# Writing the experts' gates and token numbers from GpSimd's queue instead of SyncE's

## Chip, cores and metric

The kernel runs on one core of a Trainium2 chip. The metric is the device time of one execution in microseconds (us); lower is better. The core has five engines that run their own instruction streams in order: PE (TensorE, matrix products), DVE (VectorE), ACT (ScalarE), POOL (GpSimd) and SP (SyncE, which here only starts transfers). SP and POOL can both start DMA transfers; an instruction that waits for a semaphore holds up everything behind it on its engine.

## What is computed

Three layers in a row: a linear attention with decays, a mixture of experts that sends each token to one of eight experts, and a dense layer of two matrices.

```python
for t in range(S):                                   # S = 768, 4 x 8 heads of 48
    state = alpha[:, :, t, :, None] * state + einsum('bhd,bhe->bhde', k[:, :, t], v[:, :, t])
    y[:, :, t] = einsum('bhd,bhde->bhe', q[:, :, t], state)
x = y.transpose(0, 2, 1, 3).reshape(3072, 384)
...
expert_idx = argmax(logits, axis=1)                  # logits from normalized x and expert_emb
gate_w = probs[arange(N), expert_idx]
for e in range(8):
    mask = expert_idx == e
    h = maximum(x[mask] @ w1[e], 0.0)                # 384 -> 1024
    out[mask] = gate_w[mask, None] * (h @ w2[e])     # 1024 -> 384
...
h = x @ w_in                                         # 384 -> 2048
return maximum(0.01 * h, h) @ w_out                  # 2048 -> 384
```

## The kernel before

Matrix products run in float16 with each float32 operand split into a high and a low half (`w1h`, `w1l` and so on), so that a product of two operands is three matmuls.

**Attention** (up to about 178 us) also routes: each token's row of 388 floats (its features, a norm, its gate, its token number) is scattered by POOL (L598) into `bucket`, an array in HBM with one region for each expert. The weights of expert 0 are loaded and split there too.

**The scheduled experts' stage** (about 178 to 426 us) treats 432 tokens of each expert, e = 0 to 7. For each expert:

- `gather(e)` (L834, L831): SP fetches the rows from `bucket` into `xg`, of which there are two buffers, xg0 for even experts (printed xg_1923) and xg1 for odd ones (xg_1924). So gather(e+2) must wait until all readers of expert e's rows are through.
- `put_meta(e)` (L848 to L851): two columns of `xg`, gate and token number, are written to `meta` in HBM, at a place that a register holds (`offi`, the experts' offsets, loaded by L848). The first transfer writes 384 rows of 8 bytes, the second the last 48. Since the place is known only at run time, each such transfer waits until the one before it has landed; and the first one waits until the rows of `xg` have landed.
- `block(e, n)`: ACT (L882) and DVE (L883) scale and split the rows into `xs`, and SP starts DMA transposes (L885) into `xt`, also two buffers.
- `weights(e+1, j)`: eight pieces of 128 x 768 floats, each fetched by SP (L894, into one of five `wstage` buffers) and split by ACT (L899) and DVE (L900). `double` does the same with a quarter of `w_in` or `w_out`, from 64-bit floats, through L916 to L922.
- `up(e, f)`: 72 matmuls (L940 to L942), then `hh` by ACT (L945) and `hl` by DVE (L946). `down(e, d)`: 72 matmuls (L965 to L967), then `x2h` by ACT (L971) and `x2l` by DVE (L972).

The order on each engine is made ahead of time by `Plan`: every step is added with an engine, a cost, what it reads and writes, and a due time; a list scheduler places them, and the instructions are issued in the order of planned starts. A step's cost and engine thus shift all others. For transfers the plan counts bytes over a rate plus a landing time. Of the waits inside `put_meta`, between its two transfers and from one expert's to the next, the plan knows nothing.

**The dense layer** (426 us to the end) reads `meta` back once (L1018), multiplies, and scatters the rows of the output by POOL (L799).

Of the kernel before, what the change touches and what calls it, by code (L numbers as in the profile page):

```python
# [21 lines left out]
P = 128  # L22
# [3 lines left out]
D = H * HD  # L26
NT = B * S
# [7 lines left out]
CAP = 432  # L35
# [135 lines left out]
def body(ctx, tc, qT, kT, aT, v, emb, tau, w1, w2, w_in, w_out, out):  # L171
    nc = tc.nc
# [7 lines left out]
    meta = dram.tile([X2, 2], F32, name="meta")  # L180
# [21 lines left out]
    offi = const.tile([P, E], I32, name="offi")  # L202
# [68 lines left out]
    with tc.tile_pool(name="at", bufs=1) as rt, \  # L271
# [59 lines left out]
        plan = Plan()  # L331
        NU = B * NP
        V, S_, T_, G_, Q_ = "DVE", "ACT", "PE", "POOL", "SP"
# [468 lines left out]
    with tc.tile_pool(name="mx", bufs=2) as mxp, tc.tile_pool(name="mh", bufs=1) as mhp, \  # L802
# [15 lines left out]
        size = [min(P, CAP - n * P) for n in range(NB)]  # L818
        NF = CAP // P
        plan = Plan(rate=230e3, land=4.0)  # L820
        V, S_, T_, Q_ = "DVE", "ACT", "PE", "SP"
        START, TURN = 20.0, 26.4

        def begin(e):
            return START + TURN * e
# [18 lines left out]
        def put_meta(e):  # L844
            xg = xgs[e % 2]

            def go():
                so = nc.sync.value_load(offi[0:1, e:e + 1], min_val=0, max_val=NT)  # L848
                nc.sync.dma_start(meta[ds(so, NF * P)].rearrange("(n p) c -> p n c", p=P), xg[:, :NF, D + 1:D + 3])
                if CAP % P:  # L850
                    nc.sync.dma_start(meta[ds(so + NF * P, CAP % P)], xg[:CAP % P, NF, D + 1:D + 3])  # L851

            plan.add(Q_, 1.2, go, [("xg", e % 2)], [("meta", e)], at=begin(e) + 4)

        def first_rows(n):
            x, m = xrow[n % 3], size[n]
# [118 lines left out]
        with tc.manual_schedule():  # L975
# [19 lines left out]
            for e in range(E):  # L995
                if e:
                    add(pieces_of(e))
                for f in range(NF1):
                    up(e, f)
                    if e + 1 < E and f < NB:  # L1000
                        block(e + 1, f)
                    if f == 2:
                        put_meta(e)
                    if f == 4 and e + 2 < E:
                        gather(e + 2)
                places(e)
                for d in range(KD):
                    down(e, d)
# [60 lines left out]
    with tc.If(left > 0):  # L1069
        with tc.For_i(0, left, 1) as i, tc.tile_pool(name="ox", bufs=1) as op, \  # L1070
# [7 lines left out]
            xg = op.tile([P, AUG], F32, name="xg")  # L1078
# [51 lines left out]
```

## Time and profile before

| | us |
|---|---|
| median of 3 runs | 814.64 (813.8 to 816.43) |
| the profiled execution | 810.95 |
| its span in the trace | 809.2 |
| PE busy in the span | 769.7 (95%) |
| DVE / ACT / POOL busy | 455.8 / 338.8 / 89.3 |

The profiled execution took 1.75 us more than its span, for what lies around it. PE's busy share is near full over the whole span, and the page's row of 40 slices shows where it is not: behind the first slice, all digits under 9 but the last lie between 162 and 283 us, at the end of the attention and in the first half of the experts' stage. A matmul's duration in the trace is its way through a pipeline, longer than the distance to the next one; so counts and starts tell more than sums of durations. The granted clock of TensorE stands as a share of its full 2.4 GHz; 0.5 is its lower level, 1.2 GHz.

### The profile page before, as it was taken

What the parts mean: (1) busy time and instruction counts of PE and PEld (TensorE: products, weight loads), DVE (VectorE), ACT (ScalarE), POOL (GpSimd) and SP (SyncE); (2) the same over time, 40 slices, a digit from 0 to 9 for tenths busy, and PEclk for the clock granted to TensorE, in tenths of its full rate; (3) what the DMA queues carried; (4) which work ended last, traced back from release to release, by engine and by line L of the source; (5) the groups of instructions that cost most, each with busy time, mean ns of one, the idle gap of its engine ahead of it and who ended that gap; (6) DMA issues with size and microseconds to landing.
All of it is one profiled execution on the core that took longest, in us unless ns stands there. A gap on an engine that the chain in (4) does not pass through costs nothing.

```text
span 809.2 us, 12898 instructions
## 1 busy us (share of the span) xinstructions
PE 769.7 (95%) x5098; PEld 431.5 (53%) x5098; DVE 455.8 (56%) x784; ACT 338.8 (42%) x671; POOL 89.3 (11%) x92
## 2 busy tenths in 40 slices
PE   6999999988869799999999999999999999999996
PEld 3777767645435355555554564464465465465453
DVE  9989999747355678887876504603603602602610
ACT  1344536426244567675654404403503503512510
POOL 6121624220000000000000010010000000000000
PEclk8999999999979899999999999999999999999999
DMA  8884945325666689868600000000000000000000
GB/s 304 280 272 128 294 141 184 99 95 131 157 156 159 210 198 251 184 200 226 208 25 2 1 30 10 1 20 20 1 20 20 0 20 20 1 21 20 0 21 23
DMA packets 61666, 84.08 MB, mean 104 GB/s; under 512 B 29848, under 2 KB 40864, under 8 KB 61600
## 3 DMA queue, kind: packets, MB, share of 16 engines
q1 hardware_dynamic: 58464, 73.69, 32.8%
q0 software_dynamic: 3136, 9.50, 3.0%
q8 instruction: 42, 0.69, 0.4%
q14 instruction: 24, 0.20, 0.1%
HBM read 66.80 MB, written 11.73 MB: 97 GB/s over the span
## 4 chain that ended last, share of the span: by engine, by line
issue 45%; PE 34%; DMA 7%; DVE 6%; POOL 4%; ACT 2%; SPq 1%; POOLq 0%; DVEq 0%; ACTq 0%
PE ps L966 3%; PE ps L967 3%; PE ps L965 3%; PE ps L942 3%; PE ps L941 3%; PE ps L940 3%; PE psc L398 3%; POOL out L799 3%; PE py L417 3%; PE py L449 2%; PE pfill L338 2%; DMA xg<-bucket 2%; DMA wstage<-in_w 2%; DMA meta<-xg 1%; PE ptr L477 1%
## 5 line engine op out<-in xcount | busy, mean ns | idle before, releaser
L782 DVE SCALAR_TENSOR_TENSOR g<-ps,r 128x512 f32<-128x512 f32 x96 | 65.7, 684 | 150.3 <-ACT r L781 150.3
L794 PE MATMUL ps<-woh,gh 128*128 128x384 f16 x384 | 125.2, 326 | 0.0
L795 PE MATMUL ps<-wol,gh 128*128 128x384 f16 x384 | 125.2, 326 | 0.0
L796 PE MATMUL ps<-woh,gl 128*128 128x384 f16 x384 | 125.2, 326 | 0.0
L776 PE MATMUL ps<-x2h,wih 128*128 128x512 f16 x288 | 109.1, 379 | 1.4 <-DVE x2l L972 1.4
L777 PE MATMUL ps<-x2l,wih 128*128 128x512 f16 x288 | 109.2, 379 | 0.0
L778 PE MATMUL ps<-x2h,wil 128*128 128x512 f16 x288 | 109.2, 379 | 0.0
L786 DVE TENSOR_TENSOR gl<-g,gh 128x512 f16<-128x512 f32 x96 | 66.5, 692 | 65.4 <-ACT gh L785 65.4
L785 ACT ACTIVATE gh<-g 128x512 f16<-128x512 f32 x96 | 60.4, 629 | 82.6 <-DVE g L782 82.5
L940 PE MATMUL ps<-xt,w1h 128*128 128x432 f16 x192 | 69.0, 360 | 12.6 <-DVE hl L946 9.2
L798 ACT ACTIVATE osb<-ps,ms 128x384 f32<-128x384 f32 x24 | 13.9, 580 | 159.5 <-PE ps L796 159.5
L965 PE MATMUL ps<-hh,w2h 128*128 128x432 f16 x192 | 67.5, 351 | 2.0 <-ACT hh L945 2.0
L941 PE MATMUL ps<-xt,w1h 128*128 128x432 f16 x192 | 69.0, 359 | 0.0
L942 PE MATMUL ps<-xt,w1l 128*128 128x432 f16 x192 | 68.7, 358 | 0.0
L966 PE MATMUL ps<-hl,w2h 128*128 128x432 f16 x192 | 67.5, 351 | 1.2 <-DVE hl L946 1.2
L967 PE MATMUL ps<-hh,w2l 128*128 128x432 f16 x192 | 67.5, 351 | 0.0
L799 POOL DMA_INDIRECT out<-osb,tki x24 | 23.6, 984 | 352.1 <-ACT osb L798 345.3
L781 ACT ACTIVATE r<-ps 128x512 f32<-128x512 f32 x96 | 55.9, 583 | 10.8 <-PE ps L778 7.9
L338 PE MATMUL pfill<-busy,ones 128*128 128x512 f16 x161 | 51.4, 417 | 1.5 <-POOL ident masks.py:199 1.5
L794 PEld LDWEIGHTS <-gh 128*128 128x128 f16 x384 | 37.6, 98 | 25.1
L795 PEld LDWEIGHTS <-gh 128*128 128x128 f16 x384 | 37.6, 98 | 25.1
L796 PEld LDWEIGHTS <-gl 128*128 128x128 f16 x384 | 37.6, 98 | 24.8
(197 smaller groups left out, 1133.6 us busy)
## 6 DMA issues: line engine op xcount, KB each, us to landing
wstage<-in_w SPq DMA_DIRECT2D x64, 384.0 KB, 5.2
a<-in_aT SPq DMA_DIRECT2D x16, 387.5 KB, 3.6
k<-in_kT SPq DMA_DIRECT2D x16, 384.0 KB, 4.3
q<-in_qT SPq DMA_DIRECT2D x16, 384.0 KB, 6.4
wstage<-in_w_in SPq DMA_DIRECT2D x16, 384.0 KB, 5.1
wstage<-in_w_out SPq DMA_DIRECT2D x16, 384.0 KB, 3.6
v<-in_v SPq DMA_DIRECT2D x8, 576.0 KB, 7.9
xg<-bucket SPq DMA_DIRECT2D x7, 582.0 KB, 5.6
```

Of the source, the lines that this page charges most:

```text
L776: nc.tensor.matmul(ps, wih[:, k, fs], xh[:, k], start=k == 0, stop=False)
L777: nc.tensor.matmul(ps, wih[:, k, fs], xl[:, k], start=False, stop=False)
L778: nc.tensor.matmul(ps, wil[:, k, fs], xh[:, k], start=False, stop=k == KD - 1)
L794: nc.tensor.matmul(ps, ghs[f][:, ts], woh[:, f], start=f == 0, stop=False)
L795: nc.tensor.matmul(ps, ghs[f][:, ts], wol[:, f], start=False, stop=False)
L796: nc.tensor.matmul(ps, gls[f][:, ts], woh[:, f], start=False, stop=f == NF2 - 1)
L940: nc.tensor.matmul(ps, w1h[:, f, k], xt[:, k], start=k == 0, stop=False)
L941: nc.tensor.matmul(ps, w1h[:, f, k], xt[:, KD + k], start=False, stop=False)
L942: nc.tensor.matmul(ps, w1l[:, f, k], xt[:, k], start=False, stop=k == KD - 1)
L965: nc.tensor.matmul(ps, w2h[:, f, cols], hh, start=f == 0, stop=False)
L966: nc.tensor.matmul(ps, w2h[:, f, cols], hl, start=False, stop=False)
L967: nc.tensor.matmul(ps, w2l[:, f, cols], hh, start=False, stop=f == NF1 - 1)
```

## The change

`put_meta` is issued by POOL instead of SP: the load of the offset and both transfers. In the plan it stands on POOL with a cost of 6.0 us, where it stood on SP with 1.2 us. Nothing else is edited; what moves on other engines is the scheduler's doing.

```diff
-        V, S_, T_, Q_ = "DVE", "ACT", "PE", "SP"
+        V, S_, T_, G_, Q_ = "DVE", "ACT", "PE", "POOL", "SP"
...
             def go():
-                so = nc.sync.value_load(offi[0:1, e:e + 1], min_val=0, max_val=NT)
-                nc.sync.dma_start(meta[ds(so, NF * P)].rearrange("(n p) c -> p n c", p=P), xg[:, :NF, D + 1:D + 3])
+                so = nc.gpsimd.value_load(offi[0:1, e:e + 1], min_val=0, max_val=NT)
+                nc.gpsimd.dma_start(meta[ds(so, NF * P)].rearrange("(n p) c -> p n c", p=P), xg[:, :NF, D + 1:D + 3])
                 if CAP % P:
-                    nc.sync.dma_start(meta[ds(so + NF * P, CAP % P)], xg[:CAP % P, NF, D + 1:D + 3])
-
-            plan.add(Q_, 1.2, go, [("xg", e % 2)], [("meta", e)], at=begin(e) + 4)
+                    nc.gpsimd.dma_start(meta[ds(so + NF * P, CAP % P)], xg[:CAP % P, NF, D + 1:D + 3])
+
+            plan.add(G_, 6.0, go, [("xg", e % 2)], [("meta", e)], at=begin(e) + 4)
```

PE's order is the same in both kernels. SP's list is shorter by the eight steps, and its other steps are regrouped. Here SP before, from gather(2) (into xg_1923) through put_meta(2) to the transposes of expert 1 (xt_1926):

```order
L834 DMA xg_1923<-bucket 128x3x388
L831 DMA xg_1923<-bucket 48x388
L848 TENSOR_LOAD offi
L848 ISA x2
L849 ISA
L849 DMA meta<-xg_1923 128x3x2
L851 ISA
L851 DMA meta<-xg_1923 48x2
L885 DMA_TRANSPOSE xt_1926<-xs_1931 128x6x128
L885 DMA_TRANSPOSE xt_1926<-xs_1932 128x6x128
L885 DMA_TRANSPOSE xt_1926<-xs_1933 128x6x128
L894 DMA wstage<-in_w 128x768
```

And SP at the same place of the changed kernel, on to gather(3) (into xg_1924) and the weights behind it:

```order
L885 DMA_TRANSPOSE xt_1926<-xs_1931 128x6x128
L885 DMA_TRANSPOSE xt_1926<-xs_1932 128x6x128
L834 DMA xg_1923<-bucket 128x3x388
L831 DMA xg_1923<-bucket 48x388
L885 DMA_TRANSPOSE xt_1926<-xs_1933 128x6x128
L894 DMA wstage<-in_w 128x768
L894 DMA wstage<-in_w_in 128x768
L885 DMA_TRANSPOSE xt_1926<-xs_1934 128x6x48
L834 DMA xg_1924<-bucket 128x3x388
L831 DMA xg_1924<-bucket 48x388
L894 DMA wstage<-in_w 128x768 x2
L894 DMA wstage<-in_w_in 128x768
```

Two transposes of expert 1 now stand ahead of gather(2), and between gather(2) and the weights no write of `meta` is left.

POOL gets the steps, behind the last scatter of the attention and ahead of nothing until the dense layer; for the first two experts its list reads:

```order
L598 DMA bucket<-xb_161,slot_152 24576x388 x6
L848 TENSOR_LOAD offi
L848 ISA x2
L849 ISA
L849 DMA meta<-xg_1923 128x3x2
L851 ISA
L851 DMA meta<-xg_1923 48x2
L848 TENSOR_LOAD offi
L848 ISA x2
L849 ISA
L849 DMA meta<-xg_1924 128x3x2
L851 ISA
```

On ACT the split of expert 2's rows moves, at the end of expert 0's `up` (hh_1942 is its last hidden block, xg_1923 holds gather(2)):

```order
 L945 ACTIVATE hh_1942<-ps_1958 128x432
 L919 ACTIVATE t_1953<-t_1953 128x384
+L882 ACTIVATE xs_1931<-xg_1923 128x384
 L921 ACTIVATE wih<-t_1953 128x384
+L882 ACTIVATE xs_1932<-xg_1923 128x384
 L899 ACTIVATE w2h<-wstage 128x768
 L971 ISA
 L971 ACTIVATE x2h<-ps_1959 128x432
-L882 ACTIVATE xs_1931<-xg_1923 128x384
```

ACT now reads gather(2)'s rows before it evacuates expert 0's first `down` block (x2h), where it did so behind it.

## Rows read from the trace of the kernel before

**Rows 1.** Stretches of the experts' stage: length, then each engine's busy time (instructions).

```profile
core 0: us, PE busy (x) PEld busy (x) DVE busy (x) ACT busy (x) POOL busy (x), PEclk, DMA share, GB/s
...
216.20:242.50 26.30, 15.95 (x64) 7.23 (x63) 14.84 (x26) 13.16 (x26) 0.00 (x0) 0.74 0.72 185
242.50:290.00 47.50, 42.08 (x205) 21.09 (x204) 29.77 (x53) 24.25 (x46) 0.00 (x0) 0.89 0.75 203
290.00:425.80 135.80, 135.80 (x745) 72.78 (x744) 109.33 (x191) 90.93 (x169) 0.00 (x0) 1.00 0.68 177
```

**Rows 2.** A matmul group of the page: line, operation, tiles, count, busy, idle before.

```profile
L940 PE MATMUL ps<-xt,w1h 128*128 128x432 f16 x192 | 69.0, 360 | 12.6 <-DVE hl L946 9.2
```

**Rows 3.** PE in order of time; in brackets the idle time before and its releaser.

```profile
190.01 0.35 PE L940 MATMUL ps<-xt,w1h 128*128 128x432 f16 x1
...
219.80 0.52 PE L940 MATMUL ps<-xt,w1h 128*128 128x432 f16 x1 [3.35 <-DMA xt<-xs]
...
236.46 0.52 PE L940 MATMUL ps<-xt,w1h 128*128 128x432 f16 x1 [7.01 <-DVE hl L946]
```

**Rows 4.** ACT in order of time, ahead of those two waits.

```profile
205.23 0.52 ACT L921 ACTIVATE wih<-t 128x384 f16<-128x384 f32 x1 [0.94 <-DVE t L920]
217.42 0.84 ACT L899 ACTIVATE w2h<-wstage 128x768 f16<-128x768 f32 x1 [11.67 <-DMA wstage<-in_w]
...
233.27 0.84 ACT L899 ACTIVATE w1h<-wstage 128x768 f16<-128x768 f32 x1 [9.31 <-DMA wstage<-in_w]
```

**Rows 5.** SP's transfers in order of time: start, time to start it, line.

```profile
182.95 0.41 SPq L849 DMA_DIRECT2D meta<-xg  x1
...
199.05 2.28 SPq L834 DMA_DIRECT2D xg<-bucket  x1
201.38 0.48 SPq L831 DMA_DIRECT2D xg<-bucket  x1
205.84 0.40 SPq L849 DMA_DIRECT2D meta<-xg  x1
209.53 0.34 SPq L851 DMA_DIRECT2D meta<-xg  x1
...
214.08 0.52 SPq L894 DMA_DIRECT2D wstage<-in_w  x1
...
216.72 0.56 SPq L834 DMA_DIRECT2D xg<-bucket  x1
...
227.20 0.35 SPq L894 DMA_DIRECT2D wstage<-in_w  x1
...
239.21 0.42 SPq L834 DMA_DIRECT2D xg<-bucket  x1
```

**Rows 6.** What SP's queue waited for in 180 to 430 us: total, times, longest.

```profile
SPq L851 <- DMA meta<-xg: 31.4, 8, 6.8
...
SPq L849 <- DMA xg<-bucket: 15.5, 5, 3.9
```

**Rows 7.** Transfers: count, KB, median us from issue to landing.

```profile
xt<-xs SPq DMA_TRANSPOSE x28, 5.1
...
meta<-xg SPq DMA_DIRECT2D x8, 3.0 KB, 4.1
meta<-xg SPq DMA_DIRECT2D x8, 0.4 KB, 3.4
```

**Rows 8.** POOL's own transfers in order of time (tau: 128 rows, emb: 8 rows, scatters: 128 rows).

```profile
1.96 0.76 POOL L196 DMA_DIRECT2D tau_sb<-in_tau  x1
...
7.93 0.56 POOL L327 DMA_DIRECT2D emb_sb<-in_emb  x1
...
81.22 2.37 POOL L598 DMA_INDIRECT bucket<-xb,slot  x1 [0.17 <-issue]
...
174.81 0.96 POOL L598 DMA_INDIRECT bucket<-xb,slot  x1 [0.30 <-issue]
```

**Rows 9.** The 24 scatters of L598, from issue to landing.

```profile
DMA to landing us min/median/max: 2.6/3.7/8.5
```

## The prediction

> **What bounds the kernel now.** I read the views in this order: busy time by stretch, the matmul groups and their waits, then ACT and SP ahead of those waits, to see which wait ends last.
>
> The stretches tell where PE has room. From 290.0 to 425.8 us it is busy all the time and starts 745 matmuls, one every 135.8 / 745 = 0.1823 us, at a granted clock of 1.00, the 2.4 GHz level; ahead of that it loses time [rows 1]. The stage's matmuls are six groups (L940 to L942, L965 to L967) of 192, 1152 in all [rows 2], and the first starts at 190.01 [rows 3]. At full pace they would take 1152 x 0.1823 = 210.0 us. They take 425.8 - 190.0 = 235.8. So 25.8 us are lost, all before 290. Of these PE is idle (26.30 - 15.95) + (47.50 - 42.08) = 15.8 us [rows 1]; the other 10.0 are matmuls at the 1.2 GHz level behind the waits, which is why these stretches show a clock of 0.74 and 0.89. So a us of waiting cost 10.0 / 15.8 = 0.63 us more.
>
> The two longest waits are 3.35 us for the transposed rows of expert 1 and 7.01 us for `hl` [rows 3]. Behind both stands a late start on SP. ACT sat idle for 11.67 us until a piece of `w2` came, and later 9.31 us for a piece of `w1` [rows 4]; the first was only started at 214.08, the second at 227.20 [rows 5]. What held SP is plain in its order of time: gather(2) at 199.05, then 205.84 for the write of `meta` that waits for these rows to land, 209.53 for its second transfer that waits for the first, and only then the transposes and weights [rows 5]. Over the stage SP stood 31.4 us for first transfers of `meta` to land, and 15.5 us for gathered rows, in front of queues of transfers that needed neither [rows 6].
>
> **What is taken away.** Those 31.4 + 15.5 = 46.9 us and the starts themselves, 8 x (0.41 + 0.34) = 6 us [rows 5], leave SP. That is more than the 25.8 us that PE lost, since from 290 on SP is held too and PE loses nothing. So the gain is no sum of waits: it is at most the 25.8 us of PE.
>
> What becomes early is read from the order. The transposes of expert 1 stand ahead of or just behind gather(2), with the `w2` piece, instead of behind put_meta(2); the `w1` pieces stand behind gather(3), which no write of `meta` follows. So the question is when gather(2) and gather(3) may start, since each overwrites rows that POOL must have written out.
>
> **What is added: a chain on POOL.** Call c the time of one put_meta there: first transfer to landing, second to landing. On SP the first took on average 31.4 / 8 + 0.41 = 4.3 us to landing [rows 5, 6], the second 3.4 [rows 7]. POOL's start of a plain transfer took 0.56 us for 8 rows and 0.76 for 128 [rows 8], 0.0017 us for each row more; so 384 rows are some 1.2 us and 48 are 0.63, where SP took 0.41 and 0.34. That makes c = 4.3 + 3.4 + 0.8 + 0.3 = 8.8, say 9 us. No row shows a transfer of 384 rows started by POOL, so I keep ends. Low: POOL's start costs no more than SP's, c = 7.7. High: it costs as much as three and one of the slowest scatters, 2.37 us each beside a busy DVE (0.96 beside an idle one) [rows 8], so 7.1 and 2.4: c = 7.7 + 6.7 + 2.0 = 16.4. I take 9, because plain transfers are nearer to this than scatters. The load of the offset lies beside the landing ahead of it.
>
> The chain starts when expert 0's rows are there, at 182.95 [rows 5]. Then gather(2) may start at 182.95 + c = 192 (before: 199.05), gather(3) at 182.95 + 2c = 201 (before: 216.72), gather(4), whose put_meta(2) starts behind put_meta(1), at 182.95 + 3c = 210 (before: 239.21) [rows 5]. The transposes of expert 1 then start by about 201 and land 5.1 us later [rows 7], at 206; PE needs them at 216.2, where its wait began. The `w1` pieces start by about 203 instead of 227. Both waits are covered by more than their length.
>
> A new wait comes with ACT's order: it now reads gather(2)'s rows ahead of the step that ran at 205.23 [rows 4]. These rows land 205.84 - 201.38 = 4.5 us behind the gather's last transfer [rows 5], at about 197: 8 us of cover, gone if c passes 17. DVE's order shifts in the same manner. PE's order does not change, and POOL has nothing else to do until 426, where `meta` is read back long after.
>
> **What is late next.** ACT and DVE. DVE was busy 109.33 / 135.8 = 81% where PE ran at full pace and 14.84 / 26.30 = 56% in the slow stretch [rows 1]; now it must keep the first rate from the start. It has room of a fifth, but its steps run in a planned order, and one step that waits stalls those behind. I leave 3 us for it: a wait of 1.8, and 0.63 of it again at half clock. Transfers are not it: at full pace they needed 0.68 of the DMA engines, 0.72 to 0.75 in the slow stretches [rows 1].
>
> The sum: 25.8 - 3 = 23 us less. Against the profiled execution's own 810.95 that is 788; the median of the runs is 814.64, 3.7 above it, and by that I forecast 814.64 - 23 = 791.6.
>
> The Trainium skill, in DMA: Bandwidth & Descriptors, section "Issuing engines are not separate DMA queues", says that starting transfers on several engines only saves the sequencer's time to start them, usually little. By that the 6 us of starts would be all, PE would see none of it, and the time would be 814.6. Rows 6 speak against it: here what the queue loses is not the start but the wait in front of it.
>
> **The rivals.** *Partly*: c between about 13 and 17, from slow starts on POOL. Then SP stands at gather(3) until 182.95 + 2c = 209 to 217, where it stood until 216.72 before, but without the 4 to 5 us of `meta` waits behind it. One of the two large waits stays, with what follows at half clock: 3.35 x 1.63 = 5.5 or 7.01 x 1.63 = 11.4 us off the 23, so 797 to 803, and up to 810 where, toward c = 17, both stay (5.5 + 11.4 = 16.9). For it: DVE is busy beside POOL, as in the slow scatters. Against: POOL's plain starts took 0.56 and 0.76.
>
> *No change*: that the gain sits elsewhere. If PE's early loss came from too little prefetch and not from SP, the waits for data would stay where they are: 814.6. For it: from 290 on SP is held by `meta` too, and PE loses nothing. Against: each long wait leads through ACT to a start on SP that stood behind `meta`. That the steps did not move is excluded by the order: POOL has all eight.
>
> *Slower*: POOL's chain becomes what paces the gathers. The point is c = (239.21 - 182.95) / 3 = 18.8, where gather(4) starts no earlier than before. If each transfer lands as late as the slowest scatter, 8.5 us [rows 9], and the 384 rows cost 7.1 us instead of that scatter's 2.4, c = 2 x 8.5 + 4.7 = 21.7; gather(4) starts at 248.1, 8.9 us later, PE waits that much, and 0.63 of it more at half clock: 14.5 us, 829. Against: the median scatter landed in 3.7 us [rows 9].
>
> The Trainium skill, in SBUF — State Buffer, section "SBUF: two separate sides", has a mechanism for this: a transfer started by GpSimd needs descriptors that GpSimd writes itself, and it can't write them while VectorE holds the shared port pair; it advises the SP or ACT queue instead, which is the reverse of this change. The 2.37 against 0.96 us of rows 8 are of its kind; no row shows it in this stage.
>
> **How the numbers follow.** Forecast (788 to 796): 0.72. Partly (796 to 810): 0.13. No change: 0.06. Slower: 0.09. A measurement of this kernel tells some 0.3%, 2.4 us, from no change. Faster by more than that: 0.72 + 0.13 = 0.85; within: 0.06; slower: 0.09. The low end is all of PE's loss with nothing late next, 814.64 - 25.8 = 788.8, less 2 for the spread of runs: 786.8. The high end takes in the first half of *partly*, 802. That leaves the second half of it, no change and slower out, some 0.2.
>
> **What would show it.** Right: PE's first L940 still starts near 190 us into the span and its last L967 ends some 23 us earlier, near 403; the granted clock is 1.00 from 190 on; SP shows no waits for `meta` other than at gathers; the `w2` and `w1` pieces start by 205. POOL's chain, from a first transfer's start to the next expert's, is 9 us where nothing else holds it. Wrong: that chain is over 13 us, and SP waits at L834 for POOL's transfers; or ACT waits for `xs` rows ahead of `x2h`; or PE keeps waits over 2 us between 216 and 290 with SP free, which would put the loss on ACT and DVE.

## The result, and the profile after

| | before | after |
|---|---|---|
| median of the runs, us | 815.39 (813.8 to 816.43) | 792.85 (790.36 to 794.05) |
| the profiled execution / its span, us | 810.95 / 809.2 | 791.78 / 790.2 |
| first L940 to last L967, the experts' matmuls, us | 190.0 to 425.9 | 195.0 to 405.4 |

The changed kernel takes 0.9721 times as long (95% interval 0.9689 to 0.9754), 22.5 us less. The prediction was 791.6 us in a range of 786.8 to 802.0, and the gain came by the mechanism it gave.

The stretches of the experts' stage, where [rows 1] stand for before (length, then each engine's busy time):

```profile
core 0: us, PE busy (x) PEld busy (x) DVE busy (x) ACT busy (x) POOL busy (x), PEclk, DMA share, GB/s
195.00:216.20 21.20, 21.20 (x118) 11.35 (x116) 17.30 (x31) 14.50 (x28) 2.63 (x4) 1.00 0.81 171
216.20:242.50 26.30, 26.30 (x146) 14.09 (x145) 20.15 (x35) 17.58 (x33) 2.59 (x4) 1.00 1.04 217
242.50:290.00 47.50, 47.50 (x262) 25.49 (x261) 38.26 (x65) 33.20 (x62) 3.12 (x5) 1.00 0.89 211
...
195.00:405.30 210.30, 210.30 (x1154) 112.72 (x1152) 167.97 (x292) 140.28 (x260) 9.64 (x15) 1.00 0.79 190
```

PE's busy time is as long as each stretch, and the granted clock is 1.00 throughout. The stage's 1152 matmuls took 210.4 us where they took 235.9: all of PE's loss is gone, the idle 15.8 us and the 10 us at the lower clock level. DVE is now busy 80% from the start (167.97 / 210.30), where it was 56% in the slow stretch of before. PE's list of waits in 170 to 410 us has, of this stage, only what stands at its two ends: L862 ahead of the first matmul, L776 behind the last.

```profile
PE ps L862 <- issue: 2.9, 1, 2.9
...
PE ps L776 <- DVE x2l L972: 1.4, 1, 1.4
```

SP in order of time, for [rows 5]. This execution reached the stage 4.8 us later than the one of before (gather(0) at 182.55 instead of 177.79), so 4.8 is to be taken off to compare.

```profile
195.52 4.31 SPq L885 DMA_TRANSPOSE xt<-xs  x2
199.92 0.53 SPq L834 DMA_DIRECT2D xg<-bucket  x1
...
203.57 1.72 SPq L885 DMA_TRANSPOSE xt<-xs  x1
205.39 0.53 SPq L834 DMA_DIRECT2D xg<-bucket  x1
211.67 0.33 SPq L831 DMA_DIRECT2D xg<-bucket  x1
212.10 0.84 SPq L894 DMA_DIRECT2D wstage<-in_w  x2
...
222.09 0.38 SPq L834 DMA_DIRECT2D xg<-bucket  x1
225.54 0.33 SPq L831 DMA_DIRECT2D xg<-bucket  x1
```

The last transposes of expert 1 start at 203.57 - 4.8 = 198.8, the `w1` pieces at 207.3 where they started at 227.20, gather(3) at 200.6 instead of 216.72. Of the 46.9 us that SP had waited for `meta` and for gathered rows [rows 6], two waits at gathers are left in its list, and the longest entry now is DVE giving back the buffers of weights, which is the queue running ahead:

```profile
SPq L894 <- DVE w2l L900: 38.2, 18, 5.5
...
SPq L831 <- DMA meta<-xg: 8.7, 2, 5.7
```

ACT's waits of 11.67 and 9.31 us for pieces of weights [rows 4] have become, in its list of the stage:

```profile
ACT w1h L899 <- DMA wstage<-in_w: 1.1, 2, 0.6
```

### The profile page after: what moved, and what is told of

The parts are those of the page before. It is cut to its first block, busy times and chain, and to the rows that moved or that the text cites. A ratio compares the mean times of both kernels' runs of the same rounds, so it can differ in the third digit from the quotient of the medians.

```text
span 790.2 us, 12936 instructions
## 1 busy us (share of the span) xinstructions
PE 760.8 (96%) x5098; PEld 430.3 (54%) x5098; DVE 457.2 (58%) x784; ACT 340.1 (43%) x671; POOL 100.2 (13%) x108
## 4 chain that ended last, share of the span: by engine, by line
issue 46%; PE 40%; DVE 6%; POOL 4%; ACT 1%; DMA 1%; another core or an unknown queue 1%; POOLq 0%; ACTq 0%
PE ps L967 4%; PE ps L966 4%; PE ps L965 4%; PE ps L942 4%; PE ps L941 4%; PE ps L940 4%; POOL out L799 3%; PE psc L398 3%; PE py L417 2%; PE py L449 2%; PE pfill L338 2%; PE ptr L477 1%; DVE rc L371 1%; PE ptr L385 1%; PE pkv L428 1%
## 5 line engine op out<-in xcount | busy, mean ns | idle before, releaser
L776 PE MATMUL ps<-x2h,wih 128*128 128x512 f16 x288 | 109.1, 379 | 1.4 <-DVE x2l L972 1.4
L798 ACT ACTIVATE osb<-ps,ms 128x384 f32<-128x384 f32 x24 | 13.9, 580 | 159.4 <-PE ps L796 159.4
L940 PE MATMUL ps<-xt,w1h 128*128 128x432 f16 x192 | 66.4, 346 | 0.0
L941 PE MATMUL ps<-xt,w1h 128*128 128x432 f16 x192 | 66.4, 346 | 0.0
L942 PE MATMUL ps<-xt,w1l 128*128 128x432 f16 x192 | 66.4, 346 | 0.0
L967 PE MATMUL ps<-hh,w2l 128*128 128x432 f16 x192 | 66.4, 346 | 0.0
L794 PEld LDWEIGHTS <-gh 128*128 128x128 f16 x384 | 37.6, 98 | 25.1
L795 PEld LDWEIGHTS <-gh 128*128 128x128 f16 x384 | 37.6, 98 | 25.1
```

The source lines that it names most:

```text
L776: nc.tensor.matmul(ps, wih[:, k, fs], xh[:, k], start=k == 0, stop=False)
L794: nc.tensor.matmul(ps, ghs[f][:, ts], woh[:, f], start=f == 0, stop=False)
L795: nc.tensor.matmul(ps, ghs[f][:, ts], wol[:, f], start=False, stop=False)
L940: nc.tensor.matmul(ps, w1h[:, f, k], xt[:, k], start=k == 0, stop=False)
L941: nc.tensor.matmul(ps, w1h[:, f, k], xt[:, KD + k], start=False, stop=False)
L942: nc.tensor.matmul(ps, w1l[:, f, k], xt[:, k], start=False, stop=k == KD - 1)
```

## The experiments

Two theories stood against each other. *Waits*: the writes of `meta`, by waiting for landings at the head of SP's queue, held up transposes and weights that PE needed next. *Order*: the plan, once it believed the writes elsewhere, made a better order on SP, ACT and DVE. A third, against both, was that SP saves the starts and loads themselves. The first four kernels ran together, beside runs of before with a median of 809.42 us; the other four beside 811.42. Ratios are to those. The expectations were reckoned from the 815 us of the first runs; these runs of before are 6 and 4 us shorter, and the expected times lie too high by as much. Why they differ is not shown; it is not the stage alone, as gather(0) started at 177.7 to 177.8 us in the four traces of the first group and at 181.0 to 184.1 in those of the second.

**The changed kernel once more.**

> The changed kernel once more, beside the three variants below. Both theories: 791 to 794 us, PE without a wait in the experts' stage. Its trace also tells whether the attention, whose code is the same in both kernels, varies by some 5 us from execution to execution: gather(0) started at 177.79 us in the trace of before and at 182.55 in the trace of after. If this is chance, the start falls anywhere from 177 to 183; if the change causes it, at 182 to 183.

787.88 us, 0.9740 (0.9704 to 0.9775): under the expected 791 to 794, and within it once the 6 us are taken into account. Gather(0) started at 177.78 us in its trace. So the later start in the first trace of after is not the change's doing; over the traces of these kernels it lies between 177.70 and 184.13, and the kernel planned apart, with its writes on SP, has 177.71 in one and 180.98 in the other.

**The writes on POOL, in the order of before.**

```diff
-            plan.add(G_, 6.0, go, [("xg", e % 2)], [("meta", e)], at=begin(e) + 4)
+            plan.add(Q_, 1.2, go, [("xg", e % 2)], [("meta", e)], at=begin(e) + 4)
```

> The writes on POOL, but the plan sees them on SP with 1.2 us as before, so that PE, DVE and ACT keep the order of before and SP keeps its order without the writes. Theory (the waits of the writes held up SP's queue): nearly the whole gain, 792 to 798 us; gather(3) starts some 10 us earlier than the 216.72 of before, and no wait of PE over 3 us. Rival (the new order on SP, ACT and DVE is what helped): little gain, 808 to 815 us, with the 3.35 and 7.01 us waits of PE still there.

786.98 us, 0.9733 (0.9703 to 0.9764): the whole gain with the plan of before (as a time, under the expected 792 to 798 by less than the 6 us). Gather(3) started at 204.02 us, 12.7 us earlier than before, and PE's list has the same two waits as after:

```profile
PE ps L862 <- issue: 3.1, 1, 3.1
PE ps L776 <- DVE x2l L972: 1.4, 1, 1.4
```

**The writes on SP, in the new order.**

```diff
-            plan.add(Q_, 1.2, go, [("xg", e % 2)], [("meta", e)], at=begin(e) + 4)
+            plan.add("POOL", 6.0, go, [("xg", e % 2)], [("meta", e)], at=begin(e) + 4)
```

> The writes on SP as before, in the order that the plan makes when it believes them on POOL with 6.0 us; PE, DVE and ACT have the order of after. Theory (waits): the waits of SP for meta are back, some 30 us and more in all, and so is PE's loss: 808 to 830 us. Rival (order): 791 to 800 us.

797.16 us, 0.9860 (0.9827 to 0.9892). As a time this lies in the rival's range; with 6 us taken off both, 802 to 824 and 785 to 794, it lies in neither. The order alone brings about half, 12.3 of the 21.5 us that the changed kernel gains beside the same runs. SP waits as long for `meta` as before, and PE waits too, though less (lists of SP and of PE):

```profile
SPq L851 <- DMA meta<-xg: 34.0, 8, 6.1
```

```profile
PE ps L940 <- DVE hl L946: 4.2, 2, 3.7
PE ps L965 <- ACT hh L945: 2.8, 2, 2.6
```

Why half is seen in SP's order of time:

```profile
200.46 0.57 SPq L834 DMA_DIRECT2D xg<-bucket  x1
...
204.05 1.19 SPq L885 DMA_TRANSPOSE xt<-xs  x1
205.29 0.58 SPq L834 DMA_DIRECT2D xg<-bucket  x1
...
206.52 0.82 SPq L894 DMA_DIRECT2D wstage<-in_w  x2
...
208.96 0.40 SPq L849 DMA_DIRECT2D meta<-xg  x1
215.67 0.33 SPq L851 DMA_DIRECT2D meta<-xg  x1
```

The write of gather(2)'s rows no longer stands right behind gather(2). The transposes, gather(3) and two `w1` pieces go first; by then the rows have landed, and the first write waits for nothing of them (SP's list has no entry for it any more, where it had 15.5 us). The landing of the first write, 208.96 to 215.67, still holds the queue, but with fewer transfers behind it that PE needs soon. The two effects don't add: the order alone brings half and the move alone brings all. That each takes out waits that the other would also have covered is my reading of it.

**The writes on SP, planned apart.** The first write stands behind hidden block 2 of its expert, the second, as a step of its own with its own load of the offset, behind hidden block 6, and gather(e+2) behind that.

```diff
-            plan.add(Q_, 1.2, go, [("xg", e % 2)], [("meta", e)], at=begin(e) + 4)
+            plan.add(Q_, 0.7, go, [("xg", e % 2)], [("meta", e)], at=begin(e) + 4, size=(NF * P * 8, 5.0), after=[("h", 2, 0)])
...
+            plan.add(Q_, 0.5, go, [("xg", e % 2), ("meta", e)], [("meta", e, 1)], at=begin(e) + 8, size=(CAP % P * 8, 4.0), after=[("h", 6, 0)])
...
-                    if f == 4 and e + 2 < E:
+                    if f == 6:
+                        put_rest(e)
+                    if f == 6 and e + 2 < E:
```

> The writes on SP, as many starts and bytes as before and one load of the offset more for each expert, but planned apart: the first write behind hidden block 2 of its expert, when its rows have landed long ago, the second behind hidden block 6, some 6 us later, when the first has landed. Theory (it is the wait in front of the queue, not the queue): SP's waits for meta fall from 46.9 us to some 3.5 us at each of six gathers, PE loses at most 5 us in the stage, 792 to 799 us. Rival (what SP saves is the starts and the loads themselves, and any write on SP costs this): 808 to 816 us.

785.32 us, 0.9711 (0.9678 to 0.9743), under the expected range even with the 6 us taken off it, since PE lost nothing. The starts and loads are all still on SP, so it is not they. The plan also gave SP, ACT and DVE an order of their own here, so this kernel shows that the writes can stay on SP at no cost, and not by itself which of its changes does it. SP still waits without harm: 25.1 us for `meta` at gathers (L831) and 5.2 at the second writes (L858), 30.3 us in all where some 21 were expected, and yet PE's list shows no wait within the stage. Two rows of SP's list, then its order of time around gather(2):

```profile
SPq L831 <- DMA meta<-xg: 25.1, 6, 5.4
...
SPq L858 <- DMA meta<-xg: 5.2, 2, 3.0
```

```profile
201.35 0.50 SPq L901 DMA_DIRECT2D wstage<-in_w  x1
202.75 0.36 SPq L858 DMA_DIRECT2D meta<-xg  x1
203.17 0.41 SPq L834 DMA_DIRECT2D xg<-bucket  x1
208.02 0.33 SPq L831 DMA_DIRECT2D xg<-bucket  x1
208.44 0.37 SPq L901 DMA_DIRECT2D wstage<-in_w  x1
```

The wait of 4.4 us ahead of 208.02 comes when expert 1's transposes and its weights are under way. So the length of the waits at the head of the queue does not tell their cost: 46.9 us of them (for `meta` and rows) came with 25.5 us lost by PE before (235.9 us for the experts' matmuls against 210.4), 34.0 with 11.8 in the new order (222.2), 30.3 with nothing here. What stands behind such a wait, and how soon PE needs it, is what differs.

**POOL's chain, lengthened.** In the changed kernel the first write of each expert is cut, so that there are three landings in a row, or four, instead of two.

```diff
-                nc.gpsimd.dma_start(meta[ds(so, NF * P)].rearrange("(n p) c -> p n c", p=P), xg[:, :NF, D + 1:D + 3])
+                nc.gpsimd.dma_start(meta[ds(so, 2 * P)].rearrange("(n p) c -> p n c", p=P), xg[:, :2, D + 1:D + 3])
+                nc.gpsimd.dma_start(meta[ds(so + 2 * P, P)], xg[:, 2, D + 1:D + 3])
```

> The changed kernel with the first write of each put_meta cut in two (256 and 128 rows), so that POOL's chain has three landings for an expert instead of two; same bytes, same plan. Theory (POOL's chain sets when a gather may start): in the trace of after a landing costs about 6.2 us (c between 10.2 and 13.9 us for two), so c becomes some 18.7 us, the 18.8 at which the prediction has gather(4) start no earlier than before: gather(4) at some 239 us for a stage that starts at 178, SP waits at the gathers for 25 us and more, 800 to 812 us. Rival (the chain has room beyond that, since SP has little to do that early): 787 to 793 us.

803.62 us, 0.9890 (0.9860 to 0.9920), within the theory's range: 11.8 us of the changed kernel's gain are gone.

```diff
-                nc.gpsimd.dma_start(meta[ds(so, NF * P)].rearrange("(n p) c -> p n c", p=P), xg[:, :NF, D + 1:D + 3])
+                for n in range(NF):
+                    nc.gpsimd.dma_start(meta[ds(so + n * P, P)], xg[:, n, D + 1:D + 3])
```

> The first write cut in three, four landings for an expert, c about 25 us. Theory: gather(4) starts at 182.95 + 3 x 25 = 258 us, 19 us later than before; PE waits that much and 0.63 of it more at half clock, 31 us: 825 to 845 us, slower than the kernel before. Rival (chain of no account): under 800 us.

823.55 us, 1.0136 (1.0109 to 1.0163): slower than before by 12.1 us. The experts' matmuls took 242.2 us (193.5 to 435.8), 6.3 more than before and 31.8 more than in the changed kernel; another 2.8 us stand behind the last scatter (below); the remaining 3 us lie outside both. The time lies 1.5 us under the expected range, and in it once that is lowered by 4 us, but not by the reckoning given: a landing took some 5.1 us and not 6.2, so that gather(4) started at 242.57 us, 238.1 with the later start of the stage taken off, no later than the 239.21 of before. PE's long waits came later too, at 276 to 281 and at 308 us, so that the time came out near the range is partly luck. The path is the one of the kernel before, from SP over ACT's wait for a piece of weights to `hl` and PE; here for the first long wait (the second is 8.38 us at 308.14, behind 12.15 us of ACT):

```profile
231.12 0.84 ACT L900 ACTIVATE w2h<-wstage 128x768 f16<-128x768 f32 x1 [11.00 <-DMA wstage<-in_w]
```

```profile
235.97 0.52 PE L941 MATMUL ps<-xt,w1h 128*128 128x432 f16 x1 [9.43 <-DVE hl L947]
```

The waits of PE, and those of SP at its gathers, for three landings:

```profile
PE ps L941 <- DVE hl L947: 6.5, 3, 5.2
```

```profile
SPq L831 <- DMA meta<-xg: 21.5, 4, 6.5
SPq L834 <- DMA meta<-xg: 18.6, 5, 5.9
```

and for four:

```profile
PE ps L941 <- DVE hl L947: 17.8, 2, 9.4
```

```profile
SPq L834 <- DMA meta<-xg: 36.9, 8, 7.5
SPq L831 <- DMA meta<-xg: 20.3, 5, 4.6
```

The pace is seen in the second transfers of the gathers, here of the kernel with four landings:

```profile
206.87 0.34 SPq L831 DMA_DIRECT2D xg<-bucket  x1
...
225.48 0.33 SPq L831 DMA_DIRECT2D xg<-bucket  x1
...
245.86 0.33 SPq L831 DMA_DIRECT2D xg<-bucket  x1
...
269.81 0.34 SPq L831 DMA_DIRECT2D xg<-bucket  x1
...
288.62 0.33 SPq L831 DMA_DIRECT2D xg<-bucket  x1
```

They come (288.62 - 206.87) / 4 = 20.4 us apart; with three landings 18.3, by the same rows (201.88 to 274.89). At 18.3 the kernel is 7.8 us faster than before, at 20.4 it is 12.1 slower; a straight line between puts the point of no gain at 18.3 + 2.1 x 7.8 / 19.9 = 19.1 us. By the experts' matmuls alone (221.4 and 242.2 us against 235.9 before) the same line gives 19.8. It rests on two kernels with one trace each. The prediction had put the point at 18.8, from when the gathers of before had started.

**The two best, with more rounds.**

> The kernel with the two writes planned apart on SP again, with more rounds, to tell it from the changed kernel: it had 785.3 us against 787.9. Theory: PE is at full pace in the stage in both, and the changed kernel is 1.4 us longer behind its last scatter (8.5 against 7.1 us), so this one is faster by 1 to 3 us. Rival: no difference, within 1 us.

> The changed kernel beside the one above, with as many rounds. Theory: 1 to 3 us above it, 8.5 us from the start of the last scatter to the end of the span where the kernels with the writes on SP have 7.1. Rival: within 1 us.

790.26 us (788.63 to 791.72), 0.9737, against 791.85 us (791.55 to 795.09), 0.9755; in the first group 785.32 (784.32 to 786.52) against 787.88 (785.87 to 789.39). The writes on SP, planned apart, are 1.6 and 2.6 us faster than the changed kernel in the median, but the runs of the two overlap both times, by 0.2 and 0.7 us, so the difference is likely and not sure. About as much, 1.4 to 1.5 us, stands in the traces at the very end. The last scatter's row, and the span, of the kernel planned apart, of the changed kernel, and of the one with four landings:

```profile
779.76 0.98 POOL L799 DMA_INDIRECT out<-osb,tki  x1 [6.87 <-ACTq L1078]
```

```profile
784.82 0.98 POOL L799 DMA_INDIRECT out<-osb,tki  x1 [6.87 <-ACTq L1069]
```

```profile
811.92 0.98 POOL L799 DMA_INDIRECT out<-osb,tki  x1 [6.87 <-ACTq L1070]
```

With spans of 786.9, 793.4 and 821.8 us that is 7.1, 8.6 and 9.9 us from that start to the end.

## Why the prediction was right, step by step

- **What bounds the kernel, and the ceiling of 25.8 us.** Right. The stage's matmuls took 210.4 us against 210.0 reckoned, and nothing outside the stage became faster.
- **Both large waits of PE go, since transposes and weights start early.** Right. They started by 199 and 207 us (the later start of the stage taken off) against 201 and 203 forecast; the `w1` pieces were 2 us later than the 205 named as a sign, without harm. The kernel with the plan of before shows that relieving the queue is enough, without the new order.
- **POOL's chain, c = 9 us.** Too small; this term was mis-sized, by its landings. POOL in order of time, for [rows 8] and the first three experts:

```profile
188.56 0.83 POOL L849 DMA_DIRECT2D meta<-xg  x1 [8.04 <-DVE wil L922]
195.72 0.56 POOL L851 DMA_DIRECT2D meta<-xg  x1 [6.33 <-DMA meta<-xg]
198.73 0.78 POOL L849 DMA_DIRECT2D meta<-xg  x1 [2.45 <-DMA meta<-xg]
204.46 0.53 POOL L851 DMA_DIRECT2D meta<-xg  x1 [4.96 <-DMA meta<-xg]
211.93 0.77 POOL L849 DMA_DIRECT2D meta<-xg  x1 [6.94 <-DMA meta<-xg]
225.81 0.77 POOL L849 DMA_DIRECT2D meta<-xg  x1 [7.27 <-DMA meta<-xg]
```

  From one expert's first write to the next's it was 10.2, 13.2 and 13.9 us here. The starts were cheaper than reckoned, 0.77 and 0.53 us against 1.2 and 0.63. The landings were longer: from the first write's start to the second's 7.2 us and 5.7, where 4.3 on SP plus 0.8 for a slower start had been reckoned, and from the second's to the next expert's first 3.0, 7.5 and 7.8 (218.01 to 225.81), where 3.7 had been. Two of the three lie past the 13 us that were named as a sign of being wrong and from which *partly* was to begin. *Partly* did not come, because what counts for gather(3) is the first two together: 23.4 us and not 26, so that its second transfer went at 211.67 - 4.8 = 206.9, ahead of the 209 from which that rival reckoned. A gather's first transfer needs only the first write landed (205.39, when the second had started at 204.46), so SP's waits, 8.7 us, are at two second transfers (L831) and none at L834. So the forecast held with less room than it claimed: gather(4) started at 217 us (4.8 taken off), not 210, with 22 us in hand instead of 29.
- **The new wait on ACT for gather(2)'s rows.** Did not come about; no such entry is in ACT's list.
- **3 us left for what is late next on ACT and DVE.** Wrong: PE waits for nothing in the stage, at 80% of DVE. In its place stand 1.4 us behind the last scatter, a cost the prediction did not have. So 25.8 - 0.4 - 1.4 = 24.0 us by the traces; the runs have 22.5, with an interval from 20 to 25.4, and 21.5 and 19.6 in the later groups. That the forecast of 23 lies so near owes something to luck: 3 us too many taken off for ACT and DVE, nothing for the end.
- **The rivals.** *No change* falls by the kernel with the order of before. *Slower* named a mechanism that the lengthened chains bear out, and its point of 18.8 us lies near the 19.1 (19.8) of the line between them; c did not reach it, because POOL's starts are short, though its landings are long. Half of the gain, as in *partly*, is what three landings give, with the gathers 16.3 to 20.6 us apart and not 13 to 17.
- **The two rules of the Trainium skill.** The Trainium skill, in DMA: Bandwidth & Descriptors, "Issuing engines are not separate DMA queues", would have left 6 us of starts and no change. The kernel planned apart keeps those starts and gains all, so the trace agrees that they are worth little; what moving a transfer saves is the wait in front of it, of which that section does not speak. The Trainium skill, in SBUF — State Buffer, "SBUF: two separate sides", would have POOL's starts stretched while DVE holds the shared ports. Whether DVE's steps in this stage hold them no run shows; these rows show no stretch, with DVE busy 80% (ns least, median, most of one):

```profile
L849 POOL DMA_DIRECT2D meta<-xg x8: 768/768/831, 188.6 to 303.2; - x8
L851 POOL DMA_DIRECT2D meta<-xg x8: 527/528/563, 195.7 to 309.7; - x8
```

## What to carry to other kernels

On an engine that starts transfers, look for an instruction that waits for a landing, and read what stands behind it: the price lies in how soon the next reader needs those transfers, and the length of the wait does not tell it. Such a step can be moved to an idle queue, or left where it is and planned so late that what it waits for has landed; here both bring 20 to 24 us, and a cost model that knows the landings might find the second by itself, which was not tried. Before moving it, work out the chain that forms on the other queue and from which length on it paces the first one again; here one more landing took more than half of the gain and two more made the kernel slower.

## What the hardware showed that was not expected

- The more of these transfers POOL starts, the longer the end of the run. From the last scatter's start to the end of the span it is 7.1 us in the kernels with no write of `meta` on POOL (two traces of the kernel planned apart, that of before, that of the writes on SP in the new order), 8.5 to 8.6 with 16 writes, 9.4 with 24 (the kernel with three landings, last scatter at 793.90 of 803.3) and 9.9 with 32: some 0.09 us for each, though they had landed hundreds of microseconds before. What does this at the end no run here shows.
- A plain transfer costs POOL 0.53 us to start for 48 rows, 0.55 for 128, 0.73 for 256 and 0.77 for 384, from the rows of the kernels above: much less by the row than the 0.0017 us drawn from two transfers at the start of the kernel.
- The same writes landed later from POOL's queue than from SP's: from the first write's start to the second's 5.7 to 8.4 us, 6.7 in the mean, against 3.2 to 7.4 and 4.6 before. The share of the DMA engines was also higher, 0.81 to 1.04 against 0.72 to 0.75 [rows 1]. Both may play a part. In the kernel planned apart, with the writes on SP and a share of 0.85 in 190 to 290 us, they landed 5.2 and 4.6 us behind their issue (medians), against 4.1 and 3.4 before at 0.67; in the kernel with four landings, from POOL at 0.64, writes of 128 rows took 5.3. No run changes one alone.
